# Attention sums of all four quarters of a chunk in one run, and four PSUM banks for everything else

## Chip, cores and metric

The kernel runs on one core of a Trainium2 chip. The metric is the time of one execution on the device in microseconds; lower is better. Before the change the median of four runs is 233.05 us (232.94 to 233.18).

## The reference

Input x has 2048 rows of 512 values (bf16). It is normalized row by row, and two branches use the result xn: a local attention with 32 heads of 16 values, where each row looks at itself and the seven rows 2, 4, ... 14 before it, and a gated feed-forward network with 1792 hidden columns.

```
xn = layernorm(x)
q, k, v = split(xn @ wqkv)                  # 32 heads of 16
logits[s, w] = q[s] . k[s - 2 w] / 4         # w = 0 .. 7, masked where s - 2 w < 0
o[s] = sum_w softmax_w(logits)[s, w] * v[s - 2 w]
A = o @ wo
B = (gelu(xn @ w_gate) * (xn @ w_up)) @ w_down
out = x + A * silu(B)
```

## The kernel before

The rows are worked in NJ = 4 chunks of TQ = 512. The order of all instructions is written out by hand; each engine runs its own in the order in which the program issues them, and semaphores are added where data or buffers demand them. The main loop (L480) runs for each chunk j: 14 blocks `glu(j, fc)`, then the 12 projections `qkv(j + 1, i)` of the next chunk (four tiles each of q, k, v), then four `down(j, tt)`, one for every 128 rows. The projections of chunk 0 come ahead of the loop.

- `glu` (L355): two results of 128x512, gate `g_ps` and up `u_ps`, each from four matmuls (`project`, L219); ScalarE reads one with Gelu and copies the other, VectorE multiplies them to `h`.
- `qkv` (L231): one result of four matmuls, copied by ScalarE to q, k or (through DRAM, for the shifted views `v_arr`) v.
- `down` (L368): 14 matmuls into `y_ps`, Silu by ScalarE, then four matmuls of the attention output `oT` with wo into `s_ps`, and on VectorE a product, a sum with x and the store.

The attention of a chunk is laid between these. Steps are hung on blocks by `at(key, fn, ...)` (L405) and issued by `run` just before the block of that key, in the order in which they were hung. They are:

- `qk_product` (L263), eight per chunk on VectorE, all of q with k shifted by 2w: tiles `pk`.
- `logits` (L271): 32 matmuls with 32 output columns each. Four of them, for four w, write four quarters of the partitions and run side by side. The result `L_ps` has two PSUM banks (w 0 to 3 and w 4 to 7), and ScalarE takes the exponential of both to `E`. In chunk 0 GpSimd then sets the masked places of E to zero (L288). `E` has two buffers.
- `denominators` (L290): eight 32-column matmuls sum E over w into `den_ps`; VectorE takes the reciprocal, `rs`.
- `spread_reciprocals` (L308): four 128-column matmuls into `sp_ps`, copied by ScalarE to `rb`.
- `av_product` (L319), eight per chunk on VectorE: E times v for quarter g of the 16 values of a head and half wh of the eight w: tiles `pv`. `pk` and `pv` share a pool of eight.
- `av_sums(j, gg)` (L330): 16 matmuls of 32 columns that sum four `pv` over w, for the quarters g = 2 gg and 2 gg + 1, into `o_ps` (two banks).
- `divide(j, gg)` (L345): VectorE multiplies those two quarters by `rb` into `oT`.

[...] Pool `mm` has five of one bank: all tiles with the tag "mm" take turns in them, that is `g_ps`, `u_ps`, `qkv_ps`, `y_ps`, `s_ps`, `sp_ps` and the transposes `tr` (four of them stand in the first four blocks of chunk 0). Pool `att` has one buffer each for the tag "pair" (two banks, shared by `L_ps` and `o_ps`) and for `den_ps` (one bank).

In chunks 1 to 3 logits stand at block 0, the eight products at blocks 2 to 9, denominators and the first sums at 7, spreading and the first division at 9, the second sums and division at 12. In chunk 0 logits stand at block 9; products at blocks 12 and 13 and at projections 0, 1, 3, 4, 5, 6; denominators and the first sums at projection 3, spreading at 5, the first division at 6, the second sums and division at 10. In chunk 0 and chunk 1 the `moments` of later rows (three VectorE instructions, one of GpSimd) stand in blocks 7 to 10 and 10 to 13.

Of the kernel before, what the change touches and what calls it, by code (L numbers as in the profile page):

```python
# [8 lines left out]
ALU = mybir.AluOpType  # L9
AF = mybir.ActivationFunctionType  # L10
BF16 = mybir.dt.bfloat16
F32 = mybir.dt.float32

P = 128
# [5 lines left out]
WH = 2  # L20
PAD = 16
TQ = 512
VW = TQ + WL * DIL
EPS = 1e-5
SCALE = DH ** -0.5
# [3 lines left out]
def kernel(  # L29
# [13 lines left out]
    nc = tc.nc  # L43
    B, S, D = A_x.shape
    DF = B_w_gate.shape[1]
    NT, NC, NF, NJ = S // P, D // P, DF // P, S // TQ
# [6 lines left out]
    def pool(name, bufs, **kw):  # L53
        return ctx.enter_context(tc.tile_pool(name=name, bufs=bufs, **kw))
# [10 lines left out]
    op = pool("op", 1)  # L65
# [1 line left out]
    sm2 = pool("sm2", 2)  # L67
    sm4 = pool("sm4", 4)
    dram = pool("dram", 1, space=bass.MemoryType.DRAM)
    mm = pool("mm", 5, space=bass.MemoryType.PSUM)  # L70
    att = pool("att", 1, space=bass.MemoryType.PSUM)


# [29 lines left out]
    def load_late_weights():  # L103
# [15 lines left out]
        out=vT.rearrange("(k p) n -> p k n", p=P)[:, :, 0:PAD],  # L119
        in_=warm[:, 0 : NC * PAD].rearrange("p (k n) -> p k n", k=NC),  # L120
# [108 lines left out]
    st = [dict(pk={}, pv={}) for _ in range(NJ)]  # L229
# [39 lines left out]
        st[j]["pk"][w] = pk  # L269

    def logits(j):  # L271
        L = att.tile([P, WH, TQ], F32, name="L_ps", tag="pair")
        for wh in range(WH):
            for c in range(NC):
                for wl in range(WL):
                    nc.tensor.matmul(  # L276
                        L[H * wl : H * (wl + 1), wh, :],
                        lhsT=dsum[:, c, :],
                        rhs=st[j]["pk"][WL * wh + wl][:, c, :],
                        start=(c == 0),  # L280
                        stop=(c == NC - 1),
                    )
        E = st[j]["E"] = ep.tile([P, WH, TQ], BF16, name="E")
        nc.scalar.activation(out=E[:], in_=L[:], func=AF.Exp, scale=SCALE)
        if j == 0:
            for w in range(1, W):
                wh, wl = divmod(w, WL)
                nc.gpsimd.memset(E[H * wl : H * (wl + 1), wh, 0 : w * DIL], 0.0)  # L288

    def denominators(j):  # L290

        E = st[j]["E"]
        den = att.tile([P, P], F32, name="den_ps")
        for wh in range(WH):
            for q in range(4):
                nc.tensor.matmul(  # L296
                    den[H * q : H * (q + 1), :],
                    lhsT=hsum[:],
                    rhs=E[:, wh, q * P : (q + 1) * P],
                    start=(wh == 0),  # L300
                    stop=(wh == WH - 1),
                )
        rs = sm2.tile([P, P], BF16, name="rs")
        with nc.allow_low_precision(reason="as the softmax of the reference"):
            nc.vector.reciprocal(out=rs[:], in_=den[:])
        st[j]["rs"] = rs
# [20 lines left out]
        )  # L327
        st[j]["pv"][g, wh] = pv

    def av_sums(j, gg):  # L330

        o = att.tile([P, 2, TQ], F32, name="o_ps", tag="pair")
        for g in range(2):
            for wh in range(WH):
                for i in range(4):
                    nc.tensor.matmul(  # L336
                        o[H * i : H * (i + 1), g, :],
                        lhsT=hsum[:],
                        rhs=st[j]["pv"][2 * gg + g, wh][:, i, :],
                        start=(wh == 0),  # L340
                        stop=(wh == WH - 1),
                    )
        st[j]["o"] = o

    def divide(j, gg):  # L345
        if gg == 0:
            st[j]["oT"] = op.tile([P, NC, TQ], BF16, name="oT")
        nc.vector.tensor_tensor(  # L348
            out=st[j]["oT"][:, 2 * gg : 2 * gg + 2, :],
            in0=st[j]["o"][:],  # L350
            in1=st[j]["rb"][:].unsqueeze(1).to_broadcast([P, 2, TQ]),
            op=ALU.mult,
        )

    def glu(j, fc):  # L355
        g_ps = mm.tile([P, TQ], F32, name="g_ps", tag="mm")
# [48 lines left out]
    def at(key, fn, *args):  # L405
        side.setdefault(key, []).append((fn, args))
# [15 lines left out]
    for w in range(W):  # L422
        at(("glu", 0, w), qk_product, 0, w)
    at(("glu", 0, 9), logits, 0)
    for i in range(8):
        at(("glu", 0, 12 + i) if i < 2 else ("qkv", 1, (0, 1, 3, 4, 5, 6)[i - 2]),
           av_product, 0, i // 2, i % 2)
    at(("qkv", 1, 3), denominators, 0)
    at(("qkv", 1, 3), av_sums, 0, 0)
    at(("qkv", 1, 5), spread_reciprocals, 0)  # L430
    at(("qkv", 1, 6), divide, 0, 0)
    at(("qkv", 1, 10), av_sums, 0, 1)
    at(("qkv", 1, 10), divide, 0, 1)

    for j in range(1, NJ):
        for w in range(W):
            early = j > 1 and w < 3
            at(("qkv", j, 9 + w) if early else ("down", j - 1, w // 3), qk_product, j, w)
        for i in range(TPQ):
            at(("down", j - 1, i), load_v, j, [i])  # L440
        at(("glu", j, 0), logits, j)
        for i in range(8):
            at(("glu", j, 2 + i), av_product, j, i // 2, i % 2)
        at(("glu", j, 7), denominators, j)
        at(("glu", j, 7), av_sums, j, 0)
        at(("glu", j, 9), spread_reciprocals, j)
        at(("glu", j, 9), divide, j, 0)
        at(("glu", j, 12), av_sums, j, 1)
        at(("glu", j, 12), divide, j, 1)


    HT = TPQ // 2
# [66 lines left out]
```

## Time and profile before

| | us |
|---|---|
| median of 4 runs | 233.05 |
| the profiled execution | 233.18 |
| its span, first to last instruction | 231.5 |
| TensorE busy | 224.1 |
| VectorE busy | 146.5 |
| ScalarE busy | 131.7 |
| logits, 128 matmuls, recorded | 7.6 |
| attention sums, 128 matmuls, recorded | 8.5 |
| denominators, 32 matmuls, recorded | 1.2 |

The profile is of one execution, by hardware. In its lists PE is TensorE, DVE VectorE, ACT ScalarE, POOL GpSimd, SP the queue that issues most DMAs; L12 is line 12 of the kernel. Busy time of TensorE counts overlapping matmuls once, and the end of a matmul is modelled: where one matmul follows another, the distance of their starts says what each costs. A few records of matmuls are missing from the trace, so that a group of four may be counted as three. The granted TensorE clock was full throughout (1.000).

### The profile page before, as it was taken

To read this page: it belongs to the slowest core of one execution; us is meant where nothing else is said; L and a number is where in the kernel's file an instruction comes from. 1 tells how busy PE (TensorE), PEld (TensorE's weight loads), DVE (VectorE), ACT (ScalarE), POOL (GpSimd) and SP (SyncE) were. 2 spreads that over 40 slices of the span, in tenths; PEclk is the share of its full clock that TensorE was granted. 3 is DMA by queue.
4 is the path that set the end of the run, shared out by engine and by line. 5 is a ranking of instruction groups with operands and counts; after the bars stand their busy time and mean duration, and the time that the engine had idled before them with its cause. 6 is when DMAs were issued, how large, how long until landed. Compare 5 with 4: busy or idle time off the path is not lost.

```text
span 231.5 us, 3467 instructions
## 1 busy us (share of the span) xinstructions
PE 224.1 (97%) x1289; PEld 104.0 (45%) x1313; DVE 146.5 (63%) x232; ACT 131.7 (57%) x214; POOL 23.4 (10%) x64
## 2 busy tenths in 40 slices
PE   7999999999999999999999999999999999999993
PEld 2775444444444444444444444444444444444441
DVE  4593996997795198982677149951449429864132
ACT  2779879755514865756721595656742396576211
POOL 3258914100000000130000000000000000000000
PEclk9999999999999999999999999999999999999999
DMA  5999499821288211100276711100057800000001
GB/s 169 355 373 368 106 212 209 277 79 46 84 184 196 62 23 28 26 0 0 92 170 144 160 25 31 23 6 0 25 141 158 204 27 0 0 0 4 23 23 45
DMA packets 27057, 23.71 MB, mean 102 GB/s; under 512 B 6688, under 2 KB 27040, under 8 KB 27040
## 3 DMA queue, kind: packets, MB, share of 16 engines
q1 hardware_dynamic: 26896, 23.42, 38.5%
q8 instruction: 10, 0.16, 0.3%
q10 hardware_dynamic: 144, 0.07, 0.1%
q14 instruction: 7, 0.06, 0.1%
HBM read 18.22 MB, written 4.21 MB: 97 GB/s over the span
## 4 chain that ended last, share of the span: by engine, by line
PE 94%; DVE 2%; ACT 1%; DMA 1%; issue 1%; ACTq 0%
PE u_ps L221 21%; PE y_ps L371 21%; PE g_ps L221 20%; PE qkv_ps L221 18%; PE s_ps L388 6%; PE o_ps L336 3%; PE L_ps L276 3%; PE tr L190 1%; DMA x_sb<-in_A_x_dram 1%; ACT u L363 1%; DVE stats L170 1%; PE den_ps L296 0%; PE sp_ps L311 0%; DVE m L396 0%; ACT xnT L194 0%
## 5 line engine op out<-in xcount | busy, mean ns | idle before, releaser
L221 PE MATMUL u_ps<-xnT,wu_sb 128*128 128x512 bf16 x221 | 57.0, 379 | 0.2
L221 PE MATMUL g_ps<-xnT,wg_sb 128*128 128x512 bf16 x212 | 55.9, 379 | 0.8 <-issue 0.5
L371 PE MATMUL y_ps<-wd_sb,h 128*128 128x512 bf16 x220 | 50.8, 379 | 0.2
L365 DVE TENSOR_TENSOR h<-ge,u 128x512 bf16<-128x512 bf16 x56 | 23.7, 424 | 34.3 <-ACT u L363 34.0
L266 DVE TENSOR_TENSOR pk<-q_sb,k_sb 128x2048 bf16<-128x2048 bf16 x32 | 37.8, 1219 | 11.5 <-ACT k_sb L241 11.5
L221 PE MATMUL qkv_ps<-xnT,wqkv_sb 128*128 128x512 bf16 (+1 forms) x219 | 42.7, 348 | 0.8 <-ACT xnT L194 0.5
L361 ACT ACTIVATE ge<-g_ps 128x512 bf16<-128x512 f32 x56 | 33.6, 601 | 14.4 <-PE g_ps L221 12.3
L363 ACT ACTIVATE u<-u_ps 128x512 bf16<-128x512 f32 x56 | 33.6, 600 | 13.9 <-PE u_ps L221 13.9
L322 DVE TENSOR_TENSOR pv<-E,v_arr 128x2048 bf16<-128x2048 bf16 x32 | 38.6, 1217 | 0.1
L379 ACT ACTIVATE sl<-y_ps 128x512 bf16<-128x512 f32 x16 | 9.6, 597 | 43.9 <-PE y_ps L371 43.9
L221 PEld LDWEIGHTS <-wu_sb 128*128 128x128 bf16 x224 | 21.9, 98 | 26.6 <-issue 0.3
L371 PEld LDWEIGHTS <-h 128*128 128x128 bf16 x224 | 21.9, 98 | 26.4
L221 PEld LDWEIGHTS <-wg_sb 128*128 128x128 bf16 x224 | 20.8, 98 | 26.7 <-issue 4.2
L221 PEld LDWEIGHTS <-wqkv_sb 128*128 128x128 bf16 x224 | 21.6, 98 | 19.9 <-issue 1.3
L396 DVE TENSOR_TENSOR m<-s_ps,sl 128x512 bf16<-128x512 f32 (+1 forms) x17 | 11.2, 657 | 26.6 <-PE s_ps L388 24.1
L175 POOL TENSOR_TENSOR rstd<-rstd,mhalf 128x1 f32<-128x1 f32 x16 | 10.4, 652 | 78.6 <-DVE rstd L172 78.6
L388 PE MATMUL s_ps<-wo_sb,oT 128*128 128x512 bf16 (+1 forms) x68 | 16.4, 366 | 0.0
L170 DVE BATCH_NORM_STATS2 stats<-x_sb 128x6 f32<-128x512 bf16 x16 | 11.0, 687 | 3.9 <-DMA x_sb<-in_A_x_dram 3.9
L238 ACT ACTIVATE q_sb<-qkv_ps 128x512 bf16<-128x512 f32 (+1 forms) x20 | 10.2, 512 | 5.4 <-PE qkv_ps L221 5.1
L244 ACT ACTIVATE vst<-qkv_ps 128x512 bf16<-128x512 f32 x16 | 9.6, 597 | 5.6 <-PE qkv_ps L221 4.2
L241 ACT ACTIVATE k_sb<-qkv_ps 128x512 bf16<-128x512 f32 (+1 forms) x20 | 10.2, 512 | 3.2 <-PE qkv_ps L221 2.9
L348 DVE TENSOR_TENSOR oT<-o_ps,rb 128x1024 bf16<-128x1024 f32 x8 | 9.7, 1218 | 1.4 <-PE o_ps L336 1.4
(42 smaller groups left out, 111.1 us busy)
## 6 DMA issues: line engine op xcount, KB each, us to landing
v_arr<-vT SPq DMA_DIRECT2D x16, 520.0 KB, 5.0
vT<-vst SPq DMA_DIRECT2D x16, 128.0 KB, 2.3
out_dram<-o_t SPq DMA_DIRECT2D x15, 128.0 KB, 2.3
wg_sb<-in_B_w_gate_dram SPq DMA_DIRECT2D x2, 896.0 KB
wu_sb<-in_B_w_up_dram SPq DMA_DIRECT2D x2, 896.0 KB, 13.2
wd_sb<-in_B_w_down_dram SPq DMA_DIRECT2D x1, 1792.0 KB, 17.1
wqkv_sb<-in_A_wqkv_dram SPq DMA_DIRECT2D x3, 512.0 KB, 5.5
x_sb<-in_A_x_dram SPq DMA_DIRECT2D x3, 512.0 KB, 9.9
```

The costliest lines, as they stand in the source:

```text
L170: nc.vector.bn_stats(out=stats[:, t, :], in_=x_sb[:, t, :])
L175: nc.gpsimd.tensor_tensor(out=rstd[:, t, :], in0=rstd[:, t, :], in1=mhalf[:], op=ALU.pow)
L221: nc.tensor.matmul(ps[:], lhsT=w[:, dk, lo : lo + P], rhs=xnT[j][:, dk, i0 : i0 + n], start=(dk == 0), stop=(dk == NC - 1),)
L238: nc.scalar.activation(out=st[j]["q"][:, c, i0 : i0 + n], in_=ps[:], func=AF.Copy)
L266: nc.vector.tensor_tensor(out=pk[:], in0=st[j]["q"][:], in1=k_sb[:, :, off : off + TQ], op=ALU.mult)
L322: nc.vector.tensor_tensor(out=pv[:], in0=st[j]["E"][:, wh, :].unsqueeze(1).to_broadcast([P, 4, TQ]), in1=st[j]["va"][:, 4 * g : 4 * g + 4, ...
L361: nc.scalar.activation(out=ge[:], in_=g_ps[:], func=AF.Gelu_apprx_tanh)
L363: nc.scalar.activation(out=u[:], in_=u_ps[:], func=AF.Copy)
L365: nc.vector.tensor_tensor(out=h[:], in0=ge[:], in1=u[:], op=ALU.mult)
L371: nc.tensor.matmul(y[:], lhsT=st[j][fc][:, tt * P : (tt + 1) * P], rhs=wd_sb[:, fc, :], start=(fc == 0), stop=(fc == NF - 1),)
L388: nc.tensor.matmul(s[:], lhsT=st[j]["oT"][:, g, tt * P : (tt + 1) * P], rhs=wo_sb[:, g, cols], start=(g == 0), stop=(g == NC - 1),)
L396: nc.vector.tensor_tensor(out=m[:], in0=s[:], in1=sl[:, cols], op=ALU.mult)
```

## The change

PSUM is divided anew: `mm` has four banks in place of five, and `att` one buffer of four banks, tag "quad", for `L_ps` (which uses two of them) and `o_ps`. `den_ps` has no bank of its own now, it takes its turn in `mm`.

`av_sums(j)` sums all four quarters in one run of 32 matmuls, and `divide(j)` then issues both VectorE instructions. In chunks 1 to 3 denominators and sums stand at block 11, spreading at 12, the divisions at 13. In chunk 0 the denominators stay at projection 3 and spreading at 5; all sums and both divisions stand at 10.

```diff
@@ -67,7 +67,7 @@
     sm2 = pool("sm2", 2)
     sm4 = pool("sm4", 4)
     dram = pool("dram", 1, space=bass.MemoryType.DRAM)
-    mm = pool("mm", 5, space=bass.MemoryType.PSUM)
+    mm = pool("mm", 4, space=bass.MemoryType.PSUM)
     att = pool("att", 1, space=bass.MemoryType.PSUM)
 
 
@@ -269,7 +269,7 @@
         st[j]["pk"][w] = pk
 
     def logits(j):
-        L = att.tile([P, WH, TQ], F32, name="L_ps", tag="pair")
+        L = att.tile([P, NC, TQ], F32, name="L_ps", tag="quad")
         for wh in range(WH):
             for c in range(NC):
                 for wl in range(WL):
@@ -281,7 +281,7 @@
                         stop=(c == NC - 1),
                     )
         E = st[j]["E"] = ep.tile([P, WH, TQ], BF16, name="E")
-        nc.scalar.activation(out=E[:], in_=L[:], func=AF.Exp, scale=SCALE)
+        nc.scalar.activation(out=E[:], in_=L[:, 0:WH, :], func=AF.Exp, scale=SCALE)
         if j == 0:
             for w in range(1, W):
                 wh, wl = divmod(w, WL)
@@ -290,7 +290,7 @@
     def denominators(j):
 
         E = st[j]["E"]
-        den = att.tile([P, P], F32, name="den_ps")
+        den = mm.tile([P, P], F32, name="den_ps", tag="mm")
         for wh in range(WH):
             for q in range(4):
                 nc.tensor.matmul(
@@ -327,30 +327,30 @@
         )
         st[j]["pv"][g, wh] = pv
 
-    def av_sums(j, gg):
-
-        o = att.tile([P, 2, TQ], F32, name="o_ps", tag="pair")
-        for g in range(2):
+    def av_sums(j):
+
+        o = att.tile([P, NC, TQ], F32, name="o_ps", tag="quad")
+        for g in range(NC):
             for wh in range(WH):
                 for i in range(4):
                     nc.tensor.matmul(
                         o[H * i : H * (i + 1), g, :],
                         lhsT=hsum[:],
-                        rhs=st[j]["pv"][2 * gg + g, wh][:, i, :],
+                        rhs=st[j]["pv"][g, wh][:, i, :],
                         start=(wh == 0),
                         stop=(wh == WH - 1),
                     )
         st[j]["o"] = o
 
-    def divide(j, gg):
-        if gg == 0:
-            st[j]["oT"] = op.tile([P, NC, TQ], BF16, name="oT")
-        nc.vector.tensor_tensor(
-            out=st[j]["oT"][:, 2 * gg : 2 * gg + 2, :],
-            in0=st[j]["o"][:],
-            in1=st[j]["rb"][:].unsqueeze(1).to_broadcast([P, 2, TQ]),
-            op=ALU.mult,
-        )
+    def divide(j):
+        oT = st[j]["oT"] = op.tile([P, NC, TQ], BF16, name="oT")
+        for g in range(0, NC, 2):
+            nc.vector.tensor_tensor(
+                out=oT[:, g : g + 2, :],
+                in0=st[j]["o"][:, g : g + 2, :],
+                in1=st[j]["rb"][:].unsqueeze(1).to_broadcast([P, 2, TQ]),
+                op=ALU.mult,
+            )
 
     def glu(j, fc):
         g_ps = mm.tile([P, TQ], F32, name="g_ps", tag="mm")
@@ -426,11 +426,9 @@
         at(("glu", 0, 12 + i) if i < 2 else ("qkv", 1, (0, 1, 3, 4, 5, 6)[i - 2]),
            av_product, 0, i // 2, i % 2)
     at(("qkv", 1, 3), denominators, 0)
-    at(("qkv", 1, 3), av_sums, 0, 0)
     at(("qkv", 1, 5), spread_reciprocals, 0)
-    at(("qkv", 1, 6), divide, 0, 0)
-    at(("qkv", 1, 10), av_sums, 0, 1)
-    at(("qkv", 1, 10), divide, 0, 1)
+    at(("qkv", 1, 10), av_sums, 0)
+    at(("qkv", 1, 10), divide, 0)
 
     for j in range(1, NJ):
         for w in range(W):
@@ -441,12 +439,10 @@
         at(("glu", j, 0), logits, j)
         for i in range(8):
             at(("glu", j, 2 + i), av_product, j, i // 2, i % 2)
-        at(("glu", j, 7), denominators, j)
-        at(("glu", j, 7), av_sums, j, 0)
-        at(("glu", j, 9), spread_reciprocals, j)
-        at(("glu", j, 9), divide, j, 0)
-        at(("glu", j, 12), av_sums, j, 1)
-        at(("glu", j, 12), divide, j, 1)
+        at(("glu", j, 11), denominators, j)
+        at(("glu", j, 11), av_sums, j)
+        at(("glu", j, 12), spread_reciprocals, j)
+        at(("glu", j, 13), divide, j)
 
 
     HT = TPQ // 2
```

## The prediction

> **What bounds the kernel now.** I read the page first, then TensorE's timeline, then those of ScalarE and VectorE where TensorE comes near to waiting. From the page:
>
> ```profile
> PE 224.1 (97%) x1289; PEld 104.0 (45%) x1313; DVE 146.5 (63%) x232; ACT 131.7 (57%) x214; POOL 23.4 (10%) x64
> ...
> PE 94%; DVE 2%; ACT 1%; DMA 1%; issue 1%; ACTq 0%
> ```
>
> TensorE is busy for 97% of the 231.5 us span, and the chain that ended last is 94% TensorE. So a change counts only where it shortens TensorE's stream or makes it wait. In that stream a full-width 128x512 matmul follows the last after 0.216 us (four in 0.8635 us), whatever its 379 ns of recorded duration; I count in these pitches. Lines of the timelines have start, length, engine, line, operation, tiles, count.
>
> Price of a run of 32-column matmuls, from TensorE's timeline (attention sums of chunk 0, second half):
>
> ```profile
> 51.42 4.48 PE L221 MATMUL qkv_ps<-xnT,wqkv_sb 128*128 128x512 bf16 x20
> 55.83 1.05 PE L336 MATMUL o_ps<-pv,hsum 128*32 128x512 bf16 x16
> 56.81 1.90 PE L221 MATMUL qkv_ps<-xnT,wqkv_sb 128*128 128x512 bf16 x7
> 58.55 3.19 PE L371 MATMUL y_ps<-wd_sb,h 128*128 128x512 bf16 x14
> ```
>
> From 51.42 to 58.55 is 7.13 us. The work is 20 + 8 full matmuls (one record is missing) and 16 narrow ones that run four at a time, so 4 pitches: 32 x 0.2159 = 6.91. The rest, 0.22, is the price of going into narrow tiles and out again: about 0.09 before the run, 0.12 at its end, 0.01 after. The 32-matmul logits run pays the same (35.00 to 36.84 is 1.84, against 8 pitches = 1.73, plus 0.10 ahead of it), so the price is per run, not per matmul.
>
> The place where the first sums of chunk 0 stand, on TensorE:
>
> ```profile
> 48.17 0.30 PE L296 MATMUL den_ps<-E,hsum 128*32 128x128 bf16 x8
> 48.29 1.23 PE L336 MATMUL o_ps<-pv,hsum 128*32 128x512 bf16 x16
> 49.46 1.90 PE L221 MATMUL qkv_ps<-xnT,wqkv_sb 128*128 128x512 bf16 x7
> 51.20 0.39 PE L311 MATMUL sp_ps<-rs,spread 128*128 128x128 bf16 x4
> ```
>
> and on VectorE:
>
> ```profile
> 46.72 3.49 DVE L322 TENSOR_TENSOR pv<-E,v_arr 128x2048 bf16<-128x2048 bf16 x3
> 50.13 0.95 DVE L305 RECIPROCAL rs<-den_ps 128x128 bf16<-128x128 f32 x1
> ```
>
> The reader is to see that the reciprocal doesn't wait for the denominators (done by 48.5) but for three products queued ahead of it, and ends at 51.08; the matmuls that spread it start at 51.20. TensorE just fills the time between with the first half of the sums.
>
> Where PSUM is tight, TensorE in chunk 2:
>
> ```profile
> 133.15 1.03 PE L221 MATMUL u_ps<-xnT,wu_sb 128*128 128x512 bf16 x4
> 134.01 1.03 PE L221 MATMUL g_ps<-xnT,wg_sb 128*128 128x512 bf16 x4
> 135.04 1.02 PE L221 MATMUL u_ps<-xnT,wu_sb 128*128 128x512 bf16 x4
> ```
>
> and ScalarE there:
>
> ```profile
> 127.94 0.60 ACT L379 ACTIVATE sl<-y_ps 128x512 bf16<-128x512 f32 x1 [3.29 <-PE y_ps L371]
> 130.76 1.28 ACT L284 ACT_TABLE_LOAD   x1 [2.22 <-PE L_ps L276]
> 132.05 1.02 ACT L284 ACTIVATE E<-L_ps 128x1024 bf16<-128x1024 f32 x1
> 133.09 1.28 ACT L361 ACT_TABLE_LOAD   x1
> 134.39 0.60 ACT L361 ACTIVATE ge<-g_ps 128x512 bf16<-128x512 f32 x1
> ```
>
> In chunks 1 and 3 the table for the exponential loads right after the last Silu (74.04, 183.24), beside the logits. In chunk 2 the load itself stands behind the wait for the logits and starts 2.2 us late. I read the reason off the program: this E takes the buffer of chunk 0, which GpSimd's memsets wrote, so the exponential has a second wait, and the first lands ahead of the load. So the first gate bank (g0) is free only at 134.98, and the tile five places behind it waits: 135.04 instead of 134.01 + 0.8635 = 134.87, 0.16 us lost. It shows two more things: five buffers just ran out, and a bank released by ScalarE lets TensorE go 0.05 us later.
>
> **What the Trainium skill says.** "TensorEngine Tiling (Array Packing)", Key Properties: changing the tiling mode drains TensorE. The trace agrees, at 0.22 us a round trip; the page has no figure. "ScalarE: Activation LUTs", What ACT_TABLE_LOAD costs: about 1283 ns for a load, and some 1380 ns of drain with it. The trace has 1.28 us, and the exponential follows 0.01 us after its load, so I charge no drain. "PSUM — Partial Sum Buffer", The four PSUM rules: a matmul's output fits one bank, 512 fp32. So 4 general banks hold at most four 128x512 results at once, in whatever order they are handed out: this carries the two ring costs below.
>
> **The change part by part.**
>
> *Fewer runs.* In chunks 1 to 3 the denominators and both halves of the sums become one narrow run, instead of denominators with one half and the other half apart: one round trip less per chunk, 3 x 0.22 = -0.66. Chunk 0 keeps two runs (denominators alone at projection 3, all sums at 10): 0.
>
> *Chunk 0, sums moved.* Without the first half, TensorE would reach the spreading matmuls at 48.17 + 0.12 + 0.11 + 8 x 0.216 = 50.13. The reciprocal's place in VectorE's queue is unchanged, so it still ends at 51.08, with 0.05 to the start: 51.14, against 51.20 now. TensorE idles 1.0 us and gains 0.06. The 16 matmuls come later, in the second run: 4 pitches, +0.86. Sum +0.80. The divisions, now two at 1.14 us spacing after the whole run (about 57.8 to 60.2), end ahead of the output projection, which starts 3.0 us after the run's two last projections; the products of chunk 1 queued behind them move with TensorE.
>
> *Four banks, chunk 2.* Tile g2 (134.01) needs g0's bank, free at 134.98: it starts at 135.04, 1.02 late. The 0.16 at the next tile goes, since all later tiles are late enough. +0.86.
>
> *Four banks, chunk 0's start.* While four transposes of the next chunk's rows share the ring, ScalarE is backlogged by its first Gelu table:
>
> ```profile
> 19.78 1.28 ACT L361 ACT_TABLE_LOAD   x1
> 21.07 0.60 ACT L361 ACTIVATE ge<-g_ps 128x512 bf16<-128x512 f32 x1
> ```
>
> ```profile
> 21.51 1.03 PE L221 MATMUL u_ps<-xnT,wu_sb 128*128 128x512 bf16 x4
> ```
>
> That u tile is the fourth after g0, whose bank is free at 21.67: it starts at 21.72, +0.21. Later tiles there then have room (the next nearest needs 22.64 + 0.05 and starts at 22.81).
>
> *Four banks elsewhere.* I set each tile's start against the release of the fourth tile before it. The least room is 0.25 us in the first projections (10.22 against 9.97), 0.30 after chunk 0's exponential (40.31 against 40.01) and 0.36 in chunks 1 and 3 (79.48 against 79.12): no wait.
>
> *Denominators and reciprocal at block 11 of chunks 1 to 3, spreading at 12.* The denominators now hold a general bank until the reciprocal has read it; the tile that needs it (g of block 12) comes behind the spreading matmuls, which wait for that reciprocal anyway. From denominators to spreading is 0.12 + 1.84 + 1.74 = 3.7 us. On VectorE the reciprocal stands behind h of block 10 (starts 1.76 after its u tile does, as 87.25 and 89.01 in the timelines) and in chunk 1 behind one set of moments (1.34 from one h to the next with a set between, 96.27 to 97.61): it ends about 3.1 us after the denominators begin. Room 0.5, cost 0; below nothing isn't possible, and if VectorE is later by more, the excess is paid once.
>
> *Divisions at block 13.* Two in a row put h of block 13 2.28 us of VectorE later. In chunk 3 the down projection follows at once and needs that h only with its 14th matmul. Counted from the start of u of block 12: h12 at 1.76, divisions 2.10 and 3.24, h13 from 4.38 to 4.80; the 14th matmul at 3 x 0.8635 + 13 x 0.216 = 5.40. Room 0.5 (0.35 for its weight load). In chunks 1 and 2 the projections lie between. Cost 0.
>
> *No change:* logits keep two of the four banks, and their place; DMA queues keep their order.
>
> Sum: -0.66 + 0.80 + 0.86 + 0.21 = **+1.21 us**. The profiled execution took 233.18 around a span of 231.5, so 1.7 lie outside, untouched: span 232.7. The median before is 233.05, 0.13 below the profiled one: 233.05 + 1.21 = **234.26**.
>
> **The rivals.**
>
> Four banks suffice (the allocator or the waits do better than I read): -0.66 + 0.80 = +0.14, 233.2. For it: almost everywhere there is room. Against it: at 21.51 and 134.01 four unread results are in the trace.
>
> Only chunk 2 differs: if the table load gets ahead of the wait for the logits, its loss and the old 0.16 go: -0.66 + 0.80 + 0.21 - 0.16 = +0.19, 233.24. Against it: the same buffer of E is reused.
>
> More waits: VectorE late at block 12 or 13, where the room is 0.35 to 0.5 and each 0.1 beyond it is paid; with one missed by a whole division (1.14, less 0.35), +0.8: 235.05. For it: VectorE's work is bunched there.
>
> Faster: the round trips out of narrow mode cost more than the gaps show, in chunks 1 to 3. The price must pass (1.87 + 0.47) / 3 = 0.78 us each to beat 0.2%; at 0.9 it gives 232.2. Against it: the chunk from logits to logits (74.18 to 128.70, 54.52) is accounted for with 0.22 per run.
>
> **How the numbers follow.** Forecast 72%; four banks suffice or chunk 2 differs 11%; more waits 13%; faster 4%. The forecast's own range is 233.9 to 234.6 (each of four terms by 0.1, and 0.1 of run scatter). For 8 in 10 I take 233.6 to 234.8, into the third case. A measurement tells about 0.2% (0.47 us) from no change. Faster 0.04, same 0.11, slower 0.85.
>
> **What would show it.** One narrow run of 40 matmuls, about 2.0 us, in each of chunks 1 to 3; a TensorE gap of 1.0 us before the spreading matmuls of chunk 0; a gap of 1.0 us at the third gate tile of chunk 2 and of 0.2 at the second u tile of chunk 0. No gap at block 12 and none inside the last chunk's first down projection. Wrong, if TensorE's gaps in those places are missing, or if new ones stand where I found room.

## The result and the profile after

| | before | after |
|---|---|---|
| median, us | 233.09 (64 runs) | 234.29 (43 runs) |
| profiled execution, us | 233.18 | 234.28 |
| its span, us | 231.5 | 232.6 |

The ratio of after to before is 1.0051, with a 95% interval of 1.004 to 1.0061: slower by 1.2 us. The forecast was 234.26.

The page after, TensorE's busy share and the chain that ended last:

```profile
PE 223.2 (96%) x1292; PEld 104.0 (45%) x1313; DVE 146.8 (63%) x232; ACT 132.1 (57%) x214; POOL 23.2 (10%) x64
...
PE 84%; ACT 6%; DVE 6%; issue 1%; DMA 1%; POOL 1%; ACTq 0%; DVEq 0%; POOLq 0%
```

TensorE is busy for 0.9 us less than before, yet the span is 1.1 us longer. The chain, 94% TensorE before, now has stretches of ScalarE and VectorE in it. Its shares say where the chain runs, not what is lost: in the main loop TensorE waits for each of the two engines once. The list of waits of the kernel after names both (engine and line that waited, releaser, total, times, longest; its other entries lie in the first 8 us):

```profile
PE g_ps L221 <- ACT ge L361: 0.9, 1, 0.9
PE sp_ps L311 <- DVE rs L305: 0.8, 1, 0.8
```

Such a list counts idle time against the recorded 379 ns of a matmul, of which successors hide some 160 ns; seen from start to start, TensorE loses 1.00 us in front of the spreading matmuls and 1.06 in front of the gate tile. Chunk 0 in TensorE's timeline after:

```profile
48.22 0.30 PE L296 MATMUL den_ps<-E,hsum 128*32 128x128 bf16 x8
48.45 1.90 PE L221 MATMUL qkv_ps<-xnT,wqkv_sb 128*128 128x512 bf16 x7
51.18 0.40 PE L311 MATMUL sp_ps<-rs,spread 128*128 128x128 bf16 x4 [0.83 <-DVE rs L305]
51.42 4.48 PE L221 MATMUL qkv_ps<-xnT,wqkv_sb 128*128 128x512 bf16 x20
55.83 1.91 PE L336 MATMUL o_ps<-pv,hsum 128*32 128x512 bf16 x32
57.67 1.90 PE L221 MATMUL qkv_ps<-xnT,wqkv_sb 128*128 128x512 bf16 x7
59.41 3.19 PE L371 MATMUL y_ps<-wd_sb,h 128*128 128x512 bf16 x14
```

and VectorE's there:

```profile
46.77 3.49 DVE L322 TENSOR_TENSOR pv<-E,v_arr 128x2048 bf16<-128x2048 bf16 x3
50.18 0.95 DVE L305 RECIPROCAL rs<-den_ps 128x128 bf16<-128x128 f32 x1
```

Between the start of the denominators and the spreading matmuls stand only 2.0 us of work where 2.8 were. The reciprocal still ends at 51.13, 2.9 us after the denominators began, as before. So the first half of the sums, gone from here, saved almost nothing (from the denominators to the spreading are 2.96 us in place of 3.03), and it is paid in full at 55.83, where the run is 1.84 us long (to 57.67) and was 0.98.

Chunk 2 after, TensorE and ScalarE:

```profile
132.92 1.03 PE L221 MATMUL g_ps<-xnT,wg_sb 128*128 128x512 bf16 x4
133.79 1.03 PE L221 MATMUL u_ps<-xnT,wu_sb 128*128 128x512 bf16 x4
135.71 1.02 PE L221 MATMUL g_ps<-xnT,wg_sb 128*128 128x512 bf16 x4 [0.89 <-ACT ge L361]
136.56 1.03 PE L221 MATMUL u_ps<-xnT,wu_sb 128*128 128x512 bf16 x4
```

```profile
131.43 1.28 ACT L284 ACT_TABLE_LOAD   x1 [2.24 <-PE L_ps L276]
132.72 1.02 ACT L284 ACTIVATE E<-L_ps 128x1024 bf16<-128x1024 f32 x1
133.76 1.28 ACT L361 ACT_TABLE_LOAD   x1
135.06 0.60 ACT L361 ACTIVATE ge<-g_ps 128x512 bf16<-128x512 f32 x1
```

The table load was late before the change too. With four banks the third gate tile waits until the first is read (135.66) and starts 1.92 us after the up tile before it, in place of 0.86.

A smaller gap stands at the start of chunk 0's blocks, where the second up tile starts 1.07 us after its gate tile, in place of 0.86:

```profile
20.49 1.03 PE L221 MATMUL g_ps<-xnT,wg_sb 128*128 128x512 bf16 x4
21.56 1.02 PE L221 MATMUL u_ps<-xnT,wu_sb 128*128 128x512 bf16 x4
```

What the merged runs save is seen best in chunk 1, where nothing waits. From its logits to those of chunk 2, before (narrow runs only; other lines left out):

```profile
74.18 1.91 PE L276 MATMUL L_ps<-pk,dsum 128*32 128x512 bf16 x32
88.21 0.30 PE L296 MATMUL den_ps<-E,hsum 128*32 128x128 bf16 x8
88.33 1.04 PE L336 MATMUL o_ps<-pv,hsum 128*32 128x512 bf16 x16
98.26 1.05 PE L336 MATMUL o_ps<-pv,hsum 128*32 128x512 bf16 x16
128.70 1.91 PE L276 MATMUL L_ps<-pk,dsum 128*32 128x512 bf16 x32
```

and after:

```profile
75.04 1.91 PE L276 MATMUL L_ps<-pk,dsum 128*32 128x512 bf16 x32
95.98 0.30 PE L296 MATMUL den_ps<-E,hsum 128*32 128x128 bf16 x8
96.10 1.90 PE L336 MATMUL o_ps<-pv,hsum 128*32 128x512 bf16 x32
129.34 1.91 PE L276 MATMUL L_ps<-pk,dsum 128*32 128x512 bf16 x32
```

The stretch takes 54.30 us in place of 54.52, for the same matmuls.

### The profile page after: what moved, and what is told of

The parts are those of the page before. It is cut to its first block, busy times and chain, and to the rows that moved or that the text cites. A ratio compares the mean times of both kernels' runs of the same rounds, so it can differ in the third digit from the quotient of the medians.

```text
span 232.6 us, 3473 instructions
## 1 busy us (share of the span) xinstructions
PE 223.2 (96%) x1292; PEld 104.0 (45%) x1313; DVE 146.8 (63%) x232; ACT 132.1 (57%) x214; POOL 23.2 (10%) x64
## 4 chain that ended last, share of the span: by engine, by line
PE 84%; ACT 6%; DVE 6%; issue 1%; DMA 1%; POOL 1%; ACTq 0%; DVEq 0%; POOLq 0%
PE y_ps L371 21%; PE u_ps L221 18%; PE g_ps L221 17%; PE qkv_ps L221 16%; PE s_ps L388 6%; PE o_ps L336 3%; DVE pv L322 2%; PE L_ps L276 2%; ACT L361 1%; ACT u L363 1%; ACT L284 1%; DMA x_sb<-in_A_x_dram 1%; ACT E L284 1%; DVE stats L170 1%; ACT ge L361 1%
## 5 line engine op out<-in xcount | busy, mean ns | idle before, releaser
L221 PE MATMUL g_ps<-xnT,wg_sb 128*128 128x512 bf16 x215 | 56.6, 379 | 1.3 <-ACT ge L361 0.9
```

The lines of the kernel that those rows point to most:

```text
L221: nc.tensor.matmul(ps[:], lhsT=w[:, dk, lo : lo + P], rhs=xnT[j][:, dk, i0 : i0 + n], start=(dk == 0), stop=(dk == NC - 1),)
```

## The experiments

Eight kernels ran, in two groups on one chip each; the kernel before had a median of 233.04 us beside the first four and 233.06 beside the last four. "Against after" is the difference to before, less the 1.20 us of the change.

### The smaller ring alone

```diff
 (kernel before)
-    mm = pool("mm", 5, space=bass.MemoryType.PSUM)
+    mm = pool("mm", 4, space=bass.MemoryType.PSUM)
```

> The kernel before with four general PSUM banks in place of five, and nothing else (its narrow runs and its own bank for the denominators stay). Theory: the ring costs 0.86 us at the third gate tile of chunk 2 and 0.21 us at the second up tile of chunk 0, together +1.07: 234.2 us, and the two gaps stand in the trace. Rival, four banks suffice and the loss comes from the moved sums alone: no change, 233.1.

Measured 234.13 us, ratio 1.005 (1.0038 to 1.0062): +1.09. Both gaps stand in its trace. In the timeline of TensorE, at the start of chunk 0's blocks and in chunk 2:

```profile
20.84 1.03 PE L221 MATMUL g_ps<-xnT,wg_sb 128*128 128x512 bf16 x4
21.91 1.02 PE L221 MATMUL u_ps<-xnT,wu_sb 128*128 128x512 bf16 x4
```

```profile
133.55 1.03 PE L221 MATMUL u_ps<-xnT,wu_sb 128*128 128x512 bf16 x4
135.44 1.02 PE L221 MATMUL g_ps<-xnT,wg_sb 128*128 128x512 bf16 x4 [0.87 <-ACT ge L361]
```

1.07 from gate to up is 0.21 over the usual 0.86; 1.89 in chunk 2 is 1.03 over it, of which 0.16 was lost before. The rival is out: the fifth bank alone was worth about 1.1 us.

### E in fresh buffers

```diff
 (changed kernel)
-    ep = pool("ep", 2)
+    ep = pool("ep", 4)
```

> The changed kernel with four buffers for E, so that chunk 2's exponential has no wait for GpSimd beside the one for the logits. Theory: its table load gets ahead of the wait and runs beside the logits, the gap of 1.0 us in chunk 2 is gone: -1.02 against the changed kernel, 233.3 us. Rival, a ring of four is too short wherever the exponential stands: chunk 2 keeps a gap, 234.3, and chunks 1 and 3 have one too.

Measured 233.21 us, ratio 1.0012 (0.9994 to 1.003): +0.17, or -1.03 against after. ScalarE in chunk 2:

```profile
128.53 0.60 ACT L379 ACTIVATE sl<-y_ps 128x512 bf16<-128x512 f32 x1 [3.29 <-PE y_ps L371]
129.14 1.28 ACT L284 ACT_TABLE_LOAD   x1
131.33 1.02 ACT L284 ACTIVATE E<-L_ps 128x1024 bf16<-128x1024 f32 x1 [0.90 <-PE L_ps L276]
```

The load now follows the Silu at once, and the wait for the logits is on the exponential itself. No gate tile waits in any chunk. So the ring of four is long enough behind an exponential whose table came early. In the compiled programs ScalarE's instructions here differ in the waits alone: with two buffers the one for TensorE stands by itself ahead of the load and the exponential has one for GpSimd; with four the exponential has the one for TensorE and nothing stands ahead of the load. Four buffers end all reuse, but reuse alone isn't the cause: in the changed kernel chunk 3 takes the buffer of chunk 1, which GpSimd never wrote, and its load starts right behind the last Silu (184.56).

### Chunk 0's reciprocal earlier

```diff
 (changed kernel)
+    at(("qkv", 1, 0), denominators, 0)
...
-    at(("qkv", 1, 3), denominators, 0)
```

> The changed kernel with chunk 0's denominators (and so their reciprocal, on VectorE) hung on projection 0, ahead of five of its six remaining products, in place of projection 3. Theory: the spreading matmuls no longer wait, the gap of about 1.0 us is gone and nothing takes its place: 233.3 us. Rival, the 16 matmuls cost their 0.86 at the new place in any case, because VectorE's products, now later by one reciprocal, make the single run wait: 234.3.

Measured 233.26 us, ratio 1.001 (0.9999 to 1.0022): +0.22, or -0.98 against after. The reciprocal came ahead of all six remaining products, not of five: the new line stands ahead of the loop that hangs them (left out above). TensorE's timeline there:

```profile
45.76 0.30 PE L296 MATMUL den_ps<-E,hsum 128*32 128x128 bf16 x8
45.99 4.49 PE L221 MATMUL qkv_ps<-xnT,wqkv_sb 128*128 128x512 bf16 x19
50.32 0.39 PE L311 MATMUL sp_ps<-rs,spread 128*128 128x128 bf16 x4
50.54 4.48 PE L221 MATMUL qkv_ps<-xnT,wqkv_sb 128*128 128x512 bf16 x20
54.95 1.91 PE L336 MATMUL o_ps<-pv,hsum 128*32 128x512 bf16 x32
```

From the denominators to the spreading are five projections without a gap, and the run of the sums doesn't wait either: VectorE's products, each one reciprocal later, end at 54.60. In the changed kernel the loss in chunk 0 was the wait and nothing else; the 0.19 us that TensorE waited there before the change is gone as well.

### More narrow runs

```diff
 (kernel before; the eight matmuls of each quarter g in a run of their own)
-        at(("glu", j, 7), av_sums, j, 0)
+        at(("glu", j, 7), av_sums, j, 0, (0,))
+        at(("glu", j, 8), av_sums, j, 0, (1,))
...
-        at(("glu", j, 12), av_sums, j, 1)
-        at(("glu", j, 12), divide, j, 1)
+        at(("glu", j, 12), av_sums, j, 1, (0,))
+        at(("glu", j, 13), av_sums, j, 1, (1,))
+        at(("glu", j, 13), divide, j, 1)
...
```

In chunk 0 the halves stand at projections 3 and 4, 10 and 11.

> The kernel before with each half of the sums cut into two runs of eight matmuls, a block apart: eight more narrow runs in all, the same matmuls. Theory: 0.22 us for each, less 0.19 in chunk 0, where the first half waited for a product: +1.57, 234.7 us. Rival, a round trip costs far more than the gaps beside it show (0.78 us and up): +6 us or more.

Measured 234.56 us, ratio 1.007 (1.0058 to 1.0082): +1.52. The removed wait is 0.19: before, the first half at 48.29 took 1.17 us, and the second, which waits for nothing, 0.98. With it the sum is 1.71 for eight round trips, 0.21 each. The rival of a dear round trip is out, and with it the only way that the prediction saw for the change to be faster as it stands.

### Chunk 0 in one run

```diff
 (changed kernel)
-    at(("qkv", 1, 3), denominators, 0)
-    at(("qkv", 1, 5), spread_reciprocals, 0)
+    at(("qkv", 1, 10), denominators, 0)
     at(("qkv", 1, 10), av_sums, 0)
-    at(("qkv", 1, 10), divide, 0)
+    at(("qkv", 1, 11), spread_reciprocals, 0)
+    at(("down", 0, 0), divide, 0)
```

> The changed kernel with chunk 0's denominators moved behind to projection 10, in one narrow run with the sums, spreading at 11 and the divisions ahead of the first down projection. Theory: the gap of 1.0 us goes as with early denominators, and one round trip of 0.22 more: -1.2 against the changed kernel, 233.1 us. Rival: the reciprocal, now last in the chain, delays spreading or the output projection by what is gained: 233.3 or more.

Measured 233.16 us, ratio 0.9998 (0.9977 to 1.0019): +0.10, or -1.10 against after. The median is 0.06 us from the theory and 0.14 from the least that the rival allows, too little to decide between them. The trace says more (TensorE; other lines left out):

```profile
54.23 0.30 PE L296 MATMUL den_ps<-E,hsum 128*32 128x128 bf16 x8
57.06 0.39 PE L311 MATMUL sp_ps<-rs,spread 128*128 128x128 bf16 x4
58.15 3.19 PE L371 MATMUL y_ps<-wd_sb,h 128*128 128x512 bf16 x14
```

Chunk 0's down projection starts at 58.15 in place of 59.41, -1.26, of which 0.03 lay ahead of the projections. The gap and one round trip (1.00 and 0.22) are gone, and neither the spreading nor the down projection waits.

### Gelu table at the start

```diff
 (changed kernel)
     nc.vector.memset(warm[:], 0.0)
+    first = const.tile([P, 1], BF16, name="first")
+    nc.scalar.activation(out=first[:], in_=warm[:, 0:1], func=AF.Gelu_apprx_tanh)
```

> The changed kernel with a Gelu of one column as ScalarE's first activation, so that the Gelu table is loaded at the start and not at the first gate tile. Theory: the backlog of 1.28 us there goes and with it the gap at the second up tile: -0.21, 234.1 us. Rival, the gap comes from the four transposes that share the ring, not from the table: it stays, 234.3.

Measured 234.10 us, ratio 1.0046 (1.0022 to 1.007): +1.04, or -0.16 against after. The interval doesn't tell that from nothing; the trace does. The second gate and up tiles of chunk 0 are 0.86 apart, where they were 1.07 apart after the change:

```profile
20.45 1.03 PE L223 MATMUL g_ps<-xnT,wg_sb 128*128 128x512 bf16 x4
21.31 1.03 PE L223 MATMUL u_ps<-xnT,wu_sb 128*128 128x512 bf16 x4
```

ScalarE's copies ahead of the blocks run with the Gelu table, so one load is saved: 13 in place of 14.

### The kernel before with fresh buffers for E

```diff
 (kernel before)
-    ep = pool("ep", 2)
+    ep = pool("ep", 4)
```

> The kernel before with four buffers for E. Theory: with five general banks the late table load of chunk 2 cost only 0.16: 232.9 us, and the 0.16 gap is gone from the trace. Rival: the late load costs the same with five banks as with four, -1.0: 232.1.

Measured 232.89 us, ratio 0.9991 (0.9979 to 1.0002): -0.17, which the interval doesn't tell from nothing. In the trace the tiles of chunk 2 follow each other every 0.86 us, without the old gap of 0.16. So the late load was nearly free with five banks and cost 1.0 with four.

### All three together

The changed kernel with E in four buffers, chunk 0 in one run, and the Gelu table at the start, each as above.

> The changed kernel with all three: four buffers for E, chunk 0 in one narrow run at projection 10, Gelu table at the start. Theory: the three are separate in time and add up, -1.02 - 1.2 - 0.21: 231.8 us, faster than both kernels. Rival: a wait behind one of them takes back part, 232.3 or more.

Measured 231.83 us, ratio 0.9946 (0.9928 to 0.9965): -1.23 against before, -2.43 against the change. In its list of waits TensorE has none after the first projections. It beats both kernels, and by 1.06 also the kernel before with its own late load mended (232.89). That is what four round trips (0.88) and the old wait in chunk 0 (0.19) come to.

## Why the prediction was right

Each term, from the same stretches of the two profiled executions:

| step | forecast, us | measured, us | read from |
|---|---|---|---|
| one narrow run less, chunk 1 | -0.22 | -0.22 | logits to logits 54.52, 54.30 |
| the same, chunk 3 | -0.22 | -0.22 | logits to down projection 28.53, 28.31 |
| the same, chunk 2, with the ring | +0.64 | +0.68 | logits to logits 54.68, 55.36 |
| chunk 0, sums moved | +0.80 | +0.81 | denominators to down projection 10.38, 11.19 |
| chunk 0's start, ring | +0.21 | +0.20 | first transpose to logits 16.53, 16.73 |

Together +1.25 against +1.21. Ahead of these stretches the two executions differ by -0.15: the first transpose of the blocks came at 18.47 and 18.32. That arose before the first projection (7.59 and 7.43), and the two together make the +1.1 of the span.

*Fewer runs.* Right, in size too: e4 gives the price by itself, 0.21.

*Chunk 0.* Right: the reciprocal kept its place behind three products, and e3 takes the whole loss back by moving it, with the sums left where the change put them; e5 does it in another way. Shown.

*Four banks, chunk 2.* The size was right, and the reason (a second wait on the exponential, from GpSimd's memsets in the shared buffer) was only read off the program; e2 shows it by taking that wait's cause away, with chunk 3 as the case of a reused buffer without memsets. The Trainium skill's bank size ("PSUM — Partial Sum Buffer", The four PSUM rules) bounded it: four results unread, no place for a fifth. The trace agrees: the fifth tile started at 135.71, 0.05 after the first was read.

*Four banks at the start.* Shown by e1 and e6 in the trace; 0.2 is too small for the medians of e6.

*Costs taken as nothing.* In chunk 1 the reciprocal ended 3.10 us after the denominators began, as forecast, and 0.59 ahead of the spreading matmuls. In chunk 3 h of block 13 was done at 215.19; its matmul in the down projection, the 14th, comes at 213.01 + 13 x 0.216 = 215.82. The rooms of 0.25 and more in the ring held: TensorE's waits list has no other entry there.

*Rivals.* "Four banks suffice" fell with e1, "faster" with e4. "Chunk 2 differs" didn't happen by itself, but e2 makes it happen and lands 0.03 from its figure of 233.24 (233.21). "More waits" found none.

## What to carry to other kernels

Where TensorE bounds, set the start of each PSUM tile against the release of the tile as many places before it as there would be banks: a negative number is a stall, and its size is the cost, less what TensorE already lost just behind it (here 1.02 less 0.16). Work moved out of a gap between a producer and its consumer is no saving while another engine sets when the consumer may start; move the producer with it. An activation with waits on two engines can have its table load held up by one of them, as in chunk 2, so look at what else writes its output buffer.

## What the runs showed of the hardware

A run of 32-column matmuls between full-width ones costs TensorE 0.21 to 0.22 us on top of its matmuls, whether 8 stand in it (the added runs of e4), 16 (before), or 32 and 40 (after, chunks 0 and 1).

The profiled execution of the last kernel took 233.8 us, 2 above its median, for a reason at its very start:

```profile
8.12 2.74 PE L223 MATMUL qkv_ps<-xnT,wqkv_sb 128*128 128x256 bf16 x12 [1.25 <-DMA wqkv_sb<-in_A_wqkv_dram]
```

The first weights came late, TensorE idled for 1.25 us, and then 12 matmuls took 2.74 us where they took 1.47 in the execution of the changed kernel. The granted clock was 0.51 from 7.4 to 10.0 us there and 1.00 here. A wait of this length need not do that: in the execution of the smaller ring alone, TensorE idled for 1.06 us in the same place, and the 12 matmuls took 1.49 us at a clock of 1.00. What tells the two apart is not shown. From the first transpose of the blocks to the end of the span that execution is 2.5 us shorter than the changed kernel's (20.33 to 232.1 against 18.32 to 232.6), which agrees with the medians.
